# Attention on two halves of the PE array: roles exchanged once a step, and the order of the parts between

## The chip, the cores and the metric

The kernel runs on one core of one Trainium2 chip. The metric is the device time of one launch in microseconds (us), and lower is better. The core has a matrix engine (PE, with its weight loads shown apart as PEld), a vector engine (DVE), a scalar engine (ACT), GpSimd (POOL) and DMA queues, of which SP issues those of this kernel. They run at the same time and wait for each other through semaphores. The profile is of one execution.

## What is computed

One transformer block on a sequence of 2048 rows of 512: a modulation from a condition vector, a layer norm, attention with 32 query heads of 16 that share one key and one value head, a residual, a second layer norm and a gated feed-forward part of width 1792.

```python
mod = (silu(c) @ w_mod).reshape(1, 6, 1, 512)
sa, ca, ga, sb, cb, gb = ...
h = layernorm(x) * (1 + ca) + sa
q = (h @ wq)            # 32 heads of 16
k, v = h @ wk, h @ wv   # one head of 16 each
p = softmax(q @ k.T * 16 ** -0.5)
x = x + ga * (concat(p @ v) @ wo)
h = layernorm(x) * (1 + cb) + sb
x = x + gb * ((sigmoid(h @ w_gate) * (h @ w_up)) @ w_down)
```

## The kernel before

**Units and steps.** After a prologue (`PLAN`, up to line 996) the attention runs as 32 units: `units` (L544) pairs 8 blocks of 256 queries with 4 groups of 8 heads. A unit has 16 steps (`kb`, L1115), one for each block of 128 keys, so there are 512 steps. In a step the kernel computes the scores of one key block for eight heads (tiles `st`), takes Exp of them on ACT into tiles `P`, and multiplies the P of two steps earlier (`LAG` = 2) with V into one PSUM bank, `craw`, which gathers a whole unit. Beside this runs, 84 tiles ahead of 64 a unit (`A0`, L56), a second product of queries with keys (tiles `sa`), whose row maxima DVE takes; the maxima are needed for the scores of a later unit. The program's PSUM banks for these are two for `st`, three for `sa` and two for all else (`SBANKS`, L84).

**The two row halves of PE.** Query and key tiles hold two copies side by side, in partitions 0 to 63 and 64 to 127. A product for one half uses 64 rows of the array and, cut into four by `columns` (L145), its four strips of 32 columns. So one row half can compute scores while the other multiplies P with V. A step has two halves, `h` = 0 and 1 (L1128). In half `h` the products with V use rows 64`h` to 64`h`+63 (`pv`, L644; `side[0]` keeps which), and the scores use the other rows (`st_tile(i, kb, k, 1 - h)` and `a_tile`, whose odd numbers are those of rows 64 to 127). The products with V are in float32, which PE does in two rounds: 4 heads x 2 rounds = 8 `craw` matmuls a half, 16 a step.

**The order of PE's program.** All of PE's work in the loop is kept in program order (`pe` is an `Ordered`). A half issues, by `ORDER` (L57): the first `sa` tile, the first `st` tile, the products with V (`c`), the second `sa`, the second `st`; then `piece` (L1092), some terms of other work.

**The parts between.** That other work (query projections `pq`, output projection `po`, gate and up `pgu`, down `pd`) comes in couples of groups, `Couple` (L191). In its first leg group a computes with rows 0 to 63 and group c with rows 64 to 127, and in the second leg they change places, so that each group's sum over 128 rows is made in one bank. A term is one product on each row half, eight matmuls in all; `part` (L195) issues row half 0 first, then 1. `plan` and `places` (L1031) spread the terms: `RATE` 2.2 terms a half at most times, `QRATE` 0.55 and `ERATE` 1.2 earlier on; `weight` gives the last half of a unit more (`SWAP` = 5 over the rate).

**The hand-over.** Both row halves add to the one bank `craw`, and must not do so at the same time. After its products with V a half issues `hand_over` (L159): a matmul with one column of zeros (`nought`) on the rows that have just finished, in one of the four column strips in turn, which raises the semaphore `turn`. Before the next half's products with V `take_over` (L169) makes PE wait for it. In the code before, that is so at every half but a unit's first; the last half of a unit has no hand-over, since ACT then copies the bank (`unit_end`, L665, tile `cs`). A couple issues a hand-over of its own at the end of its first leg, and waits for it ahead of its second.

**What runs behind.** The maxima of a unit are finished by `max_end` and `max_rows` (L605, L612): two small reductions on DVE, a small transposing product on rows 0 to 63 of PE at the end of a step's second half, two copies on ACT, a subtraction on DVE and four DMAs from SP's queue into the query tile. The results of a unit leave by `place`, `recip` and `finish` (L680 to L712), by step counts in `defer`.

Of the kernel before, what the change touches and what calls it, by code (L numbers as in the profile page):

```python
# [26 lines left out]
NKB = S // P  # L27
# [62 lines left out]
def adaln_mqa_glu_kernel(  # L90
# [36 lines left out]
    def sbank(name):  # L127
        return psum["s"].tile([P, 512], F32, tag=name, name=name, bufs=psum["banks"][name])
# [10 lines left out]
    pe, dve, act = Ordered(nc.tensor), Ordered(nc.vector), Ordered(nc.scalar)  # L139
# [5 lines left out]
    def columns(dst, l_, r_, start, stop):  # L145
        for c_ in range(0, P, 32):
            pe.matmul(dst[c_:c_ + 32], l_[:, c_:c_ + 32], r_, start=start, stop=stop)

    turn, done, side, open_ = nc.alloc_semaphore("turn"), [0], [0], [False]
# [4 lines left out]
    def behind(later, earlier):  # L154
        tc.add_manual_dep(later.ins, earlier.ins.name,
                          mybir.DependencyInfo(mybir.DependencyClass.Sync, mybir.DependencyReason.DATA),
                          reason="a bank that Tile doesn't follow")

    def hand_over():  # L159
        g, rs = 32 * (done[0] // 2 % 4), slice(64 * side[0], 64 * side[0] + 64)  # L160
        z = pe.matmul(raw_c["c"][g:g + 32, 0:1], nought[rs], nought[rs, 0:1], start=False, stop=False)
        if not done[0]:
            behind(z, nought_set)
        done[0] += 1
        z.then_inc(turn, 1)
        tc.add_to_no_dep_group("turn", z.ins)
        tc.no_tile_sem_insts.add(z.ins.name)

    def take_over(since=None):  # L169
        pe.wait_ge(turn, done[0] if since is None else since)  # L170
# [20 lines left out]
    class Couple:  # L191
# [3 lines left out]
        def part(self, n0, n1):  # L195
            if n0 == 0:
                for g in self.gs:
                    g.open()
            m = self.gs[0].n
            for n in range(n0, n1):  # L200
                if n == m:
                    take_over(self.since)
                for j in range(2):
                    g = self.gs[j ^ (n >= m)]
                    l_, r_, *cut = g.term(n % m, slice(64 * j, 64 * j + 64))
                    columns(cut[0](g.bank) if cut else g.bank, l_, r_, n == 0, n == 2 * m - 1)
                if n == m - 1:
                    self.since = None
                    if open_[0]:
                        hand_over()  # L210
                        self.since = done[0]
            if n1 == self.n:
                for k, g in enumerate(self.gs):
                    g.end(g.bank, k == 1)
# [189 lines left out]
    V = cp.tile([P, NKB, 32], F32, name="V")  # L404
# [144 lines left out]
    Ps = {}  # L549
# [20 lines left out]
    def get_q(i):  # L570
        if i not in qps:
            b, o = units[i]
            assert (b * QU // QB, o) in qdone
            load_q(i)
        return qps[i]


    def spot(n):
        return n // 16, n // 8 % 2, n % 2, n // 2 % 4

# [19 lines left out]
    def a_tile(i, n):  # L600
        a_max(*a_product(i, n))
# [3 lines left out]
    def max_end(i):  # L605
        m16 = wp.tile([64, 32], F32, tag="m16", name="m16", bufs=4)
        for u in range(2):
            dve.tensor_reduce(m16.rearrange("p (h t u) -> p h t u", t=2, u=2)[:, :, :, u], mxs[i][64 * u:64 * u + 64],
                              axis=AX.X, op=ALU.max)
        return lambda: max_rows(i, m16)  # L610
# [17 lines left out]
        return low  # L628


    def st_tile(i, t, pr, j):
        qp = get_q(i)
        if j == 1:
            P_[pr] = P2.tile([P, 2, 512], F32, tag=f"P{pr}", name=f"P{pr}", bufs=PBUFS)
        p_ = P_[pr]
        s_ = sbank("st")
        columns(s_, kp[64 * j:64 * j + 64, t * P:(t + 1) * P], qp[64 * j:64 * j + 64, 2 * pr:2 * pr + 2].rearrange("p r q -> p (r q)"),
                True, True)
        act.activation(p_[:, j], s_, AF.Exp, scale=0.25)
        Ps[i, t, 2 * j + pr] = p_[:, j]  # L640

    def pv(i, t, j):  # L644
        c_ = raw_c["c"]
        side[0] = j
        rs = slice(64 * j, 64 * j + 64)
        if (t, j) != (0, 0):
            take_over()
        for hh in range(4):  # L650
            z = pe.matmul(c_[32 * hh:32 * hh + 32, :], V[rs, t, :], Ps[i, t, hh][rs, :],
                          start=(t == 0 and j == 0), stop=(t == NKB - 1 and j == 1))
            if (t, j, hh) == (0, 0, 0) and i > 0:
                behind(z, raw_c["out"])
        open_[0] = (t, j) != (NKB - 1, 1)
        if open_[0]:
            hand_over()
        raw_c["last"] = z
        if j == 1:
            for hh in range(4):  # L660
                del Ps[i, t, hh]
            if t == NKB - 1:
                unit_end(i)

    def unit_end(i):  # L665
        b, o = units[i]
        cs = t32("cs")
        raw_c["out"] = act.activation(cs, raw_c["c"], AF.Identity)
        behind(raw_c["out"], raw_c["last"])
        tc.declare_no_dep(raw_c["out"].ins, group="turn", reason="later matmuls into the bank stand for them")  # L670
        if i == len(units) - 1:
            last.append(cs)
            return
        lD = dr.tile([2, 8, QU], F32, tag="lD", name="lD", bufs=3)
        raw = t32("raw")
        defer(1, lambda: place(b, o, cs, lD, raw))
# [38 lines left out]
    for g in range(8):  # L715
        p_, r_, j = g // 4, g // 2 % 2, g % 2
# [65 lines left out]
    class Transposes:  # L782
        stage, n = "tr", 4

        def __init__(self, part, u):
            self.part, self.u = part, u
# [255 lines left out]
    def ready(pair, gs, i):  # L1042
        for g in gs:
            g.ready = i * NKB
        return [(pair, g) for g in gs]
# [46 lines left out]
    def piece(s, h):  # L1092
        plan(s, 2 * s + h)
        if run:
            g, n0, n1 = run.pop(0)
            if n1 > n0:
                g.part(n0, n1)


    vq = []  # L1100
    lows = []

    for i, (b, o) in enumerate(units):
        if o == 0 and b == NQ - 1:
            ends = ffn_groups(NB - 1)
            first_rows.append(Couple(*ends[0][:2]))
        if o == 0 and b % 2 == 1 and b < NQ - 1:
            blocks[b // 2] = ffn_groups(b // 2)
            wos, trs, _, es = blocks[b // 2]
            main.extend([*ready(b // 2, [Couple(*wos[:2]), trs[0], trs[2]], i), (None, len(es)), *ready(b // 2, es, i)])  # L1110
        if o == 0 and b % 2 == 0 and b > 0:
            wos, trs, gs, _ = blocks.pop(b // 2 - 1)
            gs = [Couple(*wos[2:]), trs[1], trs[3], *gs]
            main.extend([*ready(b // 2 - 1, gs[:-KEPT], i), (None, KEPT), *ready(b // 2 - 1, gs[-KEPT:], i)])
        for kb in range(NKB):  # L1115
            s = i * NKB + kb
            now[0] = s
            if kb == NKB - QLEAD - 5 and i + 2 < len(units):
                get_q(i + 2)
            late, pend[:] = pend[:], []  # L1120
            for z in [z for z in waits if z[0] <= s]:
                waits.remove(z)
                z[1]()
            rows = [max_end(*z) for z in late]
            an = A0 + 4 * s

            old, lows[:] = lows[:], []
            for h in range(2):  # L1128
                for z in ORDER:
                    k = int(z[1:] or 0)  # L1130
                    if z[0] == "a" and an + 2 * k + 1 - h < len(alist):
                        a_tile(*alist[an + 2 * k + 1 - h])
                    if z == "c" and len(vq) >= LAG:
                        pv(*vq[0], h)
                    if z[0] == "s":
                        st_tile(i, kb, k, 1 - h)
                if h == 1:
                    lows.extend(z() for z in rows)
                piece(s, h)
                if h == 0:  # L1140
                    for z in old:
                        z()
            if len(vq) >= LAG:
                vq.pop(0)
            vq.append((i, kb))
            while wdone < nw:
                if wdone < nw - 4 and (wdone + 0.5) * WSTEPS > (s + 1) * (nw - 4):
                    break
                if wdone >= nw - 4 and s < WLAST + 3 * (wdone - nw + 4):
                    break  # L1150
                wjobs[wdone]()
                wdone += 1
# [2 lines left out]
        piece(s, 1)  # L1155
    while vq:
        for n in range(2):
            pv(*vq[0], n)
        vq.pop(0)
    while waits:  # L1160
        now[0] += 1
# [55 lines left out]
```

## Time and profile before

| | us |
|---|---|
| median of 3 runs | 1693.93 |
| lowest and highest | 1693.22, 1695.38 |
| the profiled execution | 1696.61 |
| its span in the trace | 1694.8 |
| PE busy | 1657.4 (98%) |
| DVE busy | 1422.2 (84%) |
| ACT busy | 1287.2 (76%) |
| POOL busy | 610.1 (36%) |

Nearly every instruction of the loop carries line 136, that of the helper `Ordered`, so groups are told apart by their tiles: `craw<-P,V` are the products with V, `craw<-nought` the hand-overs, `sa<-kp,qp` and `st<-qp,kp` the scores, `mx<-sa` the maxima on DVE, `P<-st` the Exp on ACT. A group's row ends in its count, busy time and mean duration, and the idle time of its engine ahead of it with the releaser. A row of the view in order of time has the start, the time from there to the end of the last of its instructions, the engine, the tiles and the count; rows of different row halves and column strips overlap, and which row half a matmul uses isn't shown: it follows from the program's order and from which row half is free. The profile's durations of matmuls include their way through the array, so a row half's pace is read from the distance of starts.

### The profile page before, as it was taken

What the parts mean: (1) busy time and instruction counts of PE and PEld (TensorE: products, weight loads), DVE (VectorE), ACT (ScalarE), POOL (GpSimd) and SP (SyncE); (2) the same over time, 40 slices, a digit from 0 to 9 for tenths busy, and PEclk for the clock granted to TensorE, in tenths of its full rate; (3) what the DMA queues carried; (4) which work ended last, traced back from release to release, by engine and by line L of the source; (5) the groups of instructions that cost most, each with busy time, mean ns of one, the idle gap of its engine ahead of it and who ended that gap; (6) DMA issues with size and microseconds to landing.
All of it is one profiled execution on the core that took longest, in us unless ns stands there. A gap on an engine that the chain in (4) does not pass through costs nothing.

```text
span 1694.8 us, 88800 instructions
## 1 busy us (share of the span) xinstructions
PE 1657.4 (98%) x40227; PEld 1010.1 (60%) x40227; DVE 1422.2 (84%) x2428; ACT 1287.2 (76%) x2335; POOL 610.1 (36%) x784
## 2 busy tenths in 40 slices
PE   6999999999999999999999999999999999999998
PEld 3335555555456767666656667676667766654443
DVE  7799999999999999999999999999999999912311
ACT  5548889889888888888888888888888888884100
POOL 4432455465032442232443232223443233122423
PEclk8989999999999999999999999999999999999999
DMA  7121333321021120111121110100121110011211
GB/s 240 57 62 44 100 107 96 102 83 40 21 64 52 45 68 14 40 28 28 28 77 53 53 40 13 41 25 26 37 78 53 41 52 16 25 46 52 87 50 38
DMA packets 86726, 94.12 MB, mean 56 GB/s; under 512 B 24916, under 2 KB 65868, under 8 KB 86348
## 3 DMA queue, kind: packets, MB, share of 16 engines
q1 hardware_dynamic: 86348, 88.44, 16.7%
q8 instruction: 315, 5.16, 1.2%
q14 instruction: 63, 0.52, 0.1%
HBM read 67.82 MB, written 16.24 MB: 50 GB/s over the span
## 4 chain that ended last, share of the span: by engine, by line
PE 85%; DVE 9%; ACT 2%; DMA 1%; issue 1%; SPq 1%; POOL 1%; POOLq 0%; ACTq 0%; DVEq 0%
PE craw L136 22%; PE pgu L136 16%; PE sa L136 14%; PE st L136 12%; PE pd L136 7%; DVE mx L136 7%; PE pgu L187 5%; PE pd L187 3%; PE po L136 3%; PE pq L136 2%; ACT P L136 1%; DMA xall<-in_A_x_dram 1%; DVE st L136 1%; SPq L136 1%; DVE h2h L136 0%
## 5 line engine op out<-in xcount | busy, mean ns | idle before, releaser
L136 DVE TENSOR_REDUCE mx<-sa 128x1 f32<-128x512 f32 x2048 | 1282.8, 680 | 84.0 <-PE st L136 37.9
L136 ACT ACTIVATE P<-st 128x512 f32<-128x512 f32 x2048 | 1167.5, 597 | 215.7 <-PE st L136 150.2
L136 PE MATMUL craw<-P,V 64*32 64x512 f32 x8192 | 1093.4, 599 | 0.5 <-PE craw L136 0.2
L136 PE MATMUL sa<-kp,qp 64*32 64x512 f16 (+1 forms) x7940 | 834.1, 378 | 9.2 <-DVE mx L136 8.2
L136 PE MATMUL st<-qp,kp 64*32 64x512 f16 x8192 | 836.3, 379 | 4.3 <-ACT P L136 4.0
L136 PEld LDWEIGHTS <-kp 64*32 64x32 f16 x8192 | 337.5, 91 | 206.0 <-issue 78.3
L136 PEld LDWEIGHTS <-qp 64*32 64x32 f16 (+1 forms) x7940 | 291.7, 92 | 152.8 <-issue 73.7
L136 PE MATMUL pgu<-h2h,gw 64*32 64x512 f16 x5248 | 290.1, 376 | 0.9
L136 PEld LDWEIGHTS <-gw 64*32 64x32 f16 x7872 | 183.9, 92 | 60.2 <-issue 22.4
L136 PEld LDWEIGHTS craw<-P,V 64*32 64x32 f32 x8192 | 180.9, 105 | 18.0 <-PE craw L136 3.9
L136 PE MATMUL pgu<-h2l,gw 64*32 64x512 f16 x2624 | 177.8, 376 | 0.2 <-POOL h2l L357 0.2
L136 PE MATMUL craw<-nought 64*32 64x1 f16 x1051 | 171.3, 163 | 0.0
L898 POOL TENSOR_SCALAR th<-th 128x512 f32<-128x512 f32 x41 | 25.4, 619 | 363.5 <-ACT th L136 279.6
L136 PEld LDWEIGHTS <-nought 64*32 64x32 f16 x1051 | 97.7, 93 | 72.0 <-issue 50.9
L557 POOL MEMSET qp<- 32x1024 f16 x60 | 56.7, 944 | 86.2 <-PE st L136 67.5
L321 POOL TENSOR_SCALAR wst<-wst 128x512 f32<-128x512 f32 x46 | 28.5, 620 | 140.5 <-DMA wst<-in_B_w_up_dram 88.3
L136 PE MATMUL pd<-wdl,gh 64*32 64x512 f16 x1152 | 77.5, 376 | 0.0
L136 PE MATMUL pd<-wdh,gh 64*32 64x512 f16 x1152 | 76.6, 376 | 0.1
L136 PE MATMUL pd<-wdh,gl 64*32 64x512 f16 x1152 | 76.2, 376 | 0.0
L187 PE MATMUL pgu<-h2h,gw 128*128 128x512 f16 x240 | 71.9, 379 | 1.5 <-DVE h2h L356 1.5
L892 ACT ACTIVATE th<-pgu 128x512 f32<-128x512 f32 x15 | 9.0, 597 | 82.1 <-PE pgu L187 82.1
L136 DVE COPY u<-pgu 128x512 f32<-128x512 f32 x41 | 27.9, 681 | 49.6 <-PE pgu L136 49.1
(160 smaller groups left out, 1451.6 us busy)
## 6 DMA issues: line engine op xcount, KB each, us to landing
gw<-wD SPq DMA_DIRECT2D x56, 512.0 KB
wD<-gw SPq DMA_DIRECT2D x14, 512.0 KB
wm<-in_w_mod_dram SPq DMA_DIRECT2D x6, 1024.0 KB
qp<-qD SPq DMA_DIRECT2D x192, 32.0 KB
qD<-q SPq DMA_DIRECT2D x16, 256.0 KB
xr<-in_A_x_dram SPq DMA_DIRECT2D x16, 256.0 KB
out_dram<-ot SPq DMA_DIRECT2D x16, 256.0 KB
raw<-cs SPq DMA_DIRECT2D x248, 16.0 KB
```

The lines of the kernel that those rows point to most:

```text
L136: return (lambda *a, **k: keep(f_(*a, **k))) if pinned else f_
L187: pe.matmul(cut[0](self.bank) if cut else self.bank, l_, r_, start=(n == 0), stop=(n == self.n - 1))
L321: pool.tensor_scalar(w_, w_, SW, 0.0, op0=ALU.mult, op1=ALU.add)
L557: eng.memset(qp[j:j + 32], 0.0)
L892: act.activation(th, p_, AF.Tanh, scale=0.5 / (SH * SW))
L898: pool.tensor_scalar(th, th, 1.0, 1.0, op0=ALU.add, op1=ALU.mult)
```

## The change

In odd steps the two halves change places: `sides(t)` gives the row half of the products with V, (0, 1) in even steps and (1, 0) in odd ones. Step t ends with V on the same rows with which step t+1 begins, so the row halves change roles only between the first and the second half of a step. `hand_over` comes only after a step's first half, and `take_over` only ahead of its second. The scores follow: in each half they use the rows that V does not, so in odd steps the even-numbered `sa` tiles come first. `P` tiles are taken in a step's first half, and the first and last matmul of a unit's sum are told by the order of the halves. `Couple.part` issues, in each term, first the product of the row half that had the scores (`1 - side[0]`), then that of the other.

```diff
@@ Couple.part
-                for j in range(2):
+                for j in (1 - side[0], side[0]):
                     g = self.gs[j ^ (n >= m)]
...
+    def sides(t):
+        return (0, 1) if t % 2 == 0 else (1, 0)
...
-    def st_tile(i, t, pr, j):
+    def st_tile(i, t, pr, j, second):
         qp = get_q(i)
-        if j == 1:
+        if not second:
             P_[pr] = P2.tile([P, 2, 512], F32, tag=f"P{pr}", name=f"P{pr}", bufs=PBUFS)
...
-    def pv(i, t, j):
+    def pv(i, t, second):
         c_ = raw_c["c"]
-        side[0] = j
+        side[0] = j = sides(t)[second]
         rs = slice(64 * j, 64 * j + 64)
-        if (t, j) != (0, 0):
+        start, stop = t == 0 and not second, t == NKB - 1 and second
+        if second:
             take_over()
         for hh in range(4):
-            z = pe.matmul(c_[32 * hh:32 * hh + 32, :], V[rs, t, :], Ps[i, t, hh][rs, :],
-                          start=(t == 0 and j == 0), stop=(t == NKB - 1 and j == 1))
-            if (t, j, hh) == (0, 0, 0) and i > 0:
+            z = pe.matmul(c_[32 * hh:32 * hh + 32, :], V[rs, t, :], Ps[i, t, hh][rs, :], start=start, stop=stop)
+            if start and hh == 0 and i > 0:
                 behind(z, raw_c["out"])
-        open_[0] = (t, j) != (NKB - 1, 1)
-        if open_[0]:
+        open_[0] = not stop
+        if not second:
             hand_over()
         raw_c["last"] = z
-        if j == 1:
+        if second:
             for hh in range(4):
                 del Ps[i, t, hh]
-            if t == NKB - 1:
+            if stop:
                 unit_end(i)
...
-            for h in range(2):
+            for n, h in enumerate(sides(kb)):
                 for z in ORDER:
...
                     if z == "c" and len(vq) >= LAG:
-                        pv(*vq[0], h)
+                        pv(*vq[0], n == 1)
                     if z[0] == "s":
-                        st_tile(i, kb, k, 1 - h)
-                if h == 1:
+                        st_tile(i, kb, k, 1 - h, n == 1)
+                if n == 1:
                     lows.extend(z() for z in rows)
-                piece(s, h)
-                if h == 0:
+                piece(s, n)
+                if n == 0:
                     for z in old:
                         z()
...
         for n in range(2):
-            pv(*vq[0], n)
+            pv(*vq[0], n == 1)
```

## Prediction

> **What bounds the kernel now.** I read the page first, then the busy time by stretches, then the groups of instructions inside the longest stretch, and last the engines in order of time over two stretches of a few microseconds.
>
> ```profile
> span 1694.8 us, 88800 instructions
> PE 1657.4 (98%) x40227; PEld 1010.1 (60%) x40227; DVE 1422.2 (84%) x2428; ACT 1287.2 (76%) x2335; POOL 610.1 (36%) x784
> L136 PE MATMUL craw<-nought 64*32 64x1 f16 x1051 | 171.3, 163 | 0.0
> L136 ACT ACTIVATE cs<-craw 128x512 f32<-128x512 f32 x32 | 19.1, 596 | 8.7 <-PE craw L136 8.1
> ```
>
> PE looks full, but a PE counted as busy may have one of its two row halves idle, so the rows have to be followed singly. The stretches are cut by the kind of work beside the attention: little of it at first ("light"), much of it from 538.6 on ("heavy").
>
> ```profile
> 115.00:450.70 335.70, 329.74 (x7548) 174.97 (x7529) 323.90 (x552) 297.51 (x551) 149.38 (x191) 1.00 0.25 74
> 538.60:1504.90 966.30, 960.76 (x28223) 655.93 (x28215) 887.16 (x1489) 813.64 (x1476) 321.31 (x390) 1.00 0.14 41
> L136 PE MATMUL craw<-P,V 64*32 64x512 f32 x5377 | 719.1, 598 | 0.0
> L136 PE MATMUL st<-qp,kp 64*32 64x512 f16 x5380 | 553.1, 377 | 0.3 <-ACT P L136 0.2
> L136 PE MATMUL sa<-kp,qp 64*32 64x512 f16 x5264 | 544.5, 376 | 3.5 <-DVE mx L136 2.9 <-issue 0.5
> L136 PE MATMUL craw<-nought 64*32 64x1 f16 x700 | 114.1, 163 | 0.0
> ```
>
> The first two rows give length, then PE, PEld, DVE, ACT and POOL, and the granted clock (1.00 in both). The group rows are of the heavy stretch. A step has 16 craw matmuls, so the heavy stretch has 5377/16 = 336 steps of 966.3/336 = 2.876 us; the matmuls left over, 28223 less the four groups, are 11502, at eight to a term 4.3 terms of parts a step.
>
> Now one stretch of it in order of time, PE first and ACT after it:
>
> ```profile
> 807.52 0.41 PE L136 MATMUL sa<-kp,qp 64*32 64x512 f16 x4
> 807.60 0.63 PE L136 MATMUL craw<-P,V 64*32 64x512 f32 x4
> 807.73 0.41 PE L136 MATMUL st<-qp,kp 64*32 64x512 f16 x4
> 807.95 0.41 PE L136 MATMUL sa<-kp,qp 64*32 64x512 f16 x4
> 808.03 0.63 PE L136 MATMUL craw<-P,V 64*32 64x512 f32 x4
> 808.17 0.41 PE L136 MATMUL st<-qp,kp 64*32 64x512 f16 x4
> 808.38 0.45 PE L136 MATMUL pd<-wdl,gh 64*32 64x512 f16 x5
> 808.48 0.16 PE L136 MATMUL craw<-nought 64*32 64x1 f16 x1
> 808.48 0.40 PE L136 MATMUL pd<-wdl,gh 64*32 64x512 f16 x3
> 808.60 0.49 PE L136 MATMUL pd<-wdh,gl 64*32 64x512 f16 x8
> 808.86 0.64 PE L136 MATMUL craw<-P,V 64*32 64x512 f32 x4
> 808.89 0.42 PE L136 MATMUL sa<-kp,qp 64*32 64x512 f16 x4
> 809.10 0.42 PE L136 MATMUL st<-qp,kp 64*32 64x512 f16 x4
> ...
> 809.53 0.42 PE L136 MATMUL st<-qp,kp 64*32 64x512 f16 x4
> 809.74 0.39 PE L136 MATMUL pd<-wdh,gh 64*32 64x512 f16 x4
> 809.76 0.16 PE L136 MATMUL craw<-nought 64*32 64x1 f16 x1
> 809.77 0.40 PE L136 MATMUL pd<-wdh,gh 64*32 64x512 f16 x4
> 809.95 0.43 PE L136 MATMUL pd<-wdl,gh 64*32 64x512 f16 x8
> 810.17 0.42 PE L136 MATMUL sa<-kp,qp 64*32 64x512 f16 x4
> 810.30 0.64 PE L136 MATMUL craw<-P,V 64*32 64x512 f32 x4
> ...
> 808.19 1.26 ACT L136 ACTIVATE P<-st 128x512 f32<-128x512 f32 x2 [0.27 <-PE st L136]
> 809.63 1.14 ACT L136 ACTIVATE P<-st 128x512 f32<-128x512 f32 x2 [0.18 <-PE st L136]
> ```
>
> Score row: sa, st, sa, st start 0.215 us apart (807.52 to 808.38 is four of them), then a part of 0.215. PV row: two rounds of 0.43 (807.60, 808.03), then the hand-over matmul (nought) and the parts. So the row work of a step is 2 x 0.87 for PV, 8 x 0.215 for scores and 4.3 x 2 x 0.215 for parts, 5.31 us over two rows: 2.65 each, and 2.876 - 2.65 = 0.22 us of each step a row stands idle.
>
> Part of it is at the exchange. The score row that began at 807.52 is free at 808.60 + 0.215 = 808.815, but its PV starts at 808.86, and its first round takes 0.45 where one with weights loaded ahead takes 0.43. The hand-over was long done (808.48 + 0.16). What ends last is ACT: the first of the two Exp from 808.19 ends 0.6 later, at 808.79, and frees the bank of the next half's first st, which stands ahead of PV in the program. The next exchange is alike: free at 809.95 + 0.215 = 810.165, Exp from 809.63 to 810.23, PV at 810.30. So a score row gives way to PV **1.34** (807.52 to 808.86) or **1.41** us (808.89 to 810.30) after it began, though its work with two terms takes 6 x 0.215 = 1.29. A PV row gives way to scores after 1.31 (808.86 to 810.17), which is its work.
>
> In the light stretch the limit is another:
>
> ```profile
> 298.86 5.46 DVE L136 TENSOR_REDUCE mx<-sa 128x1 f32<-128x512 f32 x9
> L136 DVE TENSOR_REDUCE mx<-sa 128x1 f32<-128x512 f32 x512 | 314.5, 678 | 11.6 <-PE sa L136 5.1 <-PE st L136 4.7
> 303.55 0.64 PE L136 MATMUL craw<-P,V 64*32 64x512 f32 x4
> ...
> 304.28 0.40 PE L136 MATMUL st<-qp,kp 64*32 64x512 f16 x4
> 304.43 0.16 PE L136 MATMUL craw<-nought 64*32 64x1 f16 x1
> 304.44 0.40 PE L136 MATMUL sa<-kp,qp 64*32 64x512 f16 x4
> 304.86 0.40 PE L136 MATMUL st<-qp,kp 64*32 64x512 f16 x4
> 304.88 0.64 PE L136 MATMUL craw<-P,V 64*32 64x512 f32 x4
> ```
>
> DVE runs nine maxima in 5.46 us, 0.607 each, one into the other. All 512 of the light stretch need 311 us so, the rest of DVE 323.9 - 314.5 = 9.4 more: 320 of 335.7. DVE sets the pace, and PE is late for it by some 15 us in all. The rows show how: the next sa (304.44) must wait until PV has left its row (nought at 304.43), while the row that had scores stands idle from 304.28 + 0.215 to 304.88.
>
> **The change, part by part.** A step keeps its four sa, four st, 16 craw matmuls and parts; no DMA, DVE or ACT instruction is added or removed, and nothing is moved past a queue of SP or POOL.
>
> *One exchange a step instead of two, heavy stretch.* After the second half the score row goes on with scores and the PV row with PV. Per row, with two terms a half, now: 1.34 or 1.41 as score row, 1.31 as PV row, so (1.34 + 1.41 + 2 x 1.31)/4 = 1.343 a half, 2.685 a step. After: a score row takes 1.29 over the border and 1.34 or 1.41 at the exchange; a PV row 1.31 at the exchange and, over the border, 1.31 or as long as the Exp holds it (st is still ahead of PV, so PV of the new half cannot start before 1.34 to 1.41 from the beginning of the old scores; it began up to 0.09 after them, which leaves 1.31 to 1.41, say 1.34). Two steps: (1.29 + 1.34 + 1.31 + 1.34) + (1.29 + 1.41 + 1.31 + 1.34) = 10.63 over two rows and two steps: 2.658. The gain is 0.027 a step, for halves of two terms; a third term (1.51 of work) covers the wait already, and with 4.3 terms a step about one half in seven has it: 0.023 x 336 = 8 us. Of the idle 0.22, the recurrence explains only 2.685 + 0.3 x 0.215 - 2.65 = 0.10; the other 0.12 are late banks and late reductions, which at an exchange hold both rows, since each takes the other's place. Over a border they hold one. Bounds: nothing, or half of 0.12 x 336 = 20 us; I take 8, nearer the low end, because DVE (887.16 of 966.30 by the row) takes back part. Together **16**, between 0 and 37 (half of the 0.22 x 336 = 74).
>
> *The light stretch.* Over a border the next sa no longer waits for PV to leave, so half of the places where DVE starves go. Bounds 0 and 15; I take **9**, a little over half, since one half of slack also absorbs the next exchange.
>
> *Hand-over matmuls.* Of 1051, those after the second halves go: 15 in each of the 32 units, 480. Each holds one of a row's four column strips, not the row: between 808.48 and the next part in that strip lie about 0.02 us. That is 0 to 480 x 0.02 / 2 = 5 us; **2**. The wait on them goes too, at the border; at the exchange it stays. Queued behind it are sa, st and the parts of that half, as before.
>
> *Parts begin with the score row.* In the old order this was so in every second half. The score row's first part starts 0.21 after its last st either way (808.17 to 808.38, 809.53 to 809.74), so the two rows do not hold each other: **0**. If they did, the lag between the rows, 808.48 - 808.38 = 0.10, would be paid in one half a step.
>
> The Trainium skill, "TensorE: Matmul & The Clock Gate" (Part 3, what overlaps), says that matmuls start and end strictly in program order. The rows disagree: nought (808.48) stands ahead of sa (807.95) and st (808.17) in the program and starts after them. By the page's rule this part would gain up to 0.10 x 336 = 34 us; it is counted among the rivals.
>
> *Order within a step.* In odd steps the two halves change places; the maxima's four sa and the Exp come in another order, with the same counts and the same banks. At a unit's end PV's last and the next unit's first half are now on one row, and the copy of the bank (cs, 0.596) is covered as before by the five terms put there, 5 x 0.215 = 1.08: **0**; without that cover 32 x 0.6 = 19 us.
>
> *The rest* (88 us between the stretches, 47 after): **1**.
>
> Sum: 16 + 9 + 2 + 0 + 0 + 1 = 28. The profiled execution took 1696.61 us (span 1694.8); 1696.6 - 28 = 1668.6. The median of the runs, 1693.93, lies 2.7 lower, so the forecast is **1666 us**.
>
> **The rivals.** *A, the rows hold each other more than I read.* Then most of what is bounded above comes: 37 + 15 + 5 = 57, or the 34 of the part order on top of half of that: about 1637. For it: the unexplained 0.12 a step. Against: the score row's parts start on time in both orders. *B, PV is held behind scores on the border (slower).* One mechanism: over the border sa and st stand ahead of PV, and if PV's weights must wait until the score row has begun its new sa and loaded the weights of its st, PV starts about 0.12 after that sa (810.17 to 810.30 is such a distance). The PV row then loses 1.29 + 0.12 - 1.31 = 0.10 at every border whose rows lie closer than 0.12, and so does the next exchange, which waits for that row: up to 0.10 x 336 = 34, or half of it as the score row has 0.05 in hand; less the 9 and 2 above that is 6 to 23, and I take 10: 1704. It decides where the rows' lag is under 0.12. For it: 807.60 and 810.30 follow sa closely. Against: 808.86 comes ahead of sa 808.89, so PV passes scores that stand before it. *C, nothing.* ACT's Exp and DVE's maxima hold the halves as before and the saved waits only turn into waits for banks: 1692. For it: at both exchanges the Exp ended last. Against: over the border the score row needs its st bank 0.215 later than PV now feels it.
>
> **How the numbers follow.** Main case (1650 to 1685) 0.60, A 0.16, C 0.09, B 0.15. About 0.2% (3.4 us) is what a measurement can tell from no change. Faster: main, A and a quarter of C, 0.78; same: the rest of C and a little of B, 0.08; slower 0.14. The range 1640 to 1694 holds the main case, C and the nearer half of A, and leaves out B and A's far end.
>
> **What would show it.** Right: about 571 nought matmuls; heavy steps of some 2.82 us and light ones near 2.56 (now 335.7 over 512/4 = 128 steps, 2.62); at the border craw follows a part on its own row with no gap and the 0.43 spacing of its rounds; at the exchange the gap of 0.04 to 0.13 after an Exp as now. Wrong: craw at the border about 0.12 after sa with its row idle (B); DVE's maxima spaced as now with PE's gaps moved to sa (C); heavy steps under 2.75 (A). The forecast fails if the late banks, which I only bounded, make up the exchange's cost or take the gain back.

## The result, and the profile after

The changed kernel takes **1685.1 us** (median of 6 runs, 1682.68 to 1685.67), the kernel before 1695.88 (6 runs, 1693.22 to 1698.62): a ratio of 0.9933, 95% interval 0.9919 to 0.9946. It is faster, by 11 us where 28 were forecast. The page of the changed kernel, the lines that answer to those of before:

```profile
span 1683.7 us, 87854 instructions
PE 1644.5 (98%) x39747; PEld 974.6 (58%) x39747; DVE 1430.9 (85%) x2428; ACT 1295.4 (77%) x2335; POOL 610.5 (36%) x784
L136 PE MATMUL craw<-nought 64*32 64x1 f16 x571 | 93.1, 163 | 0.0
```

The change was made as described: 480 of the 1051 hand-overs are gone. The busy time by stretches, cut at the same steps as before (columns: length, then PE, PEld, DVE, ACT, POOL, the clock):

```profile
115.58:449.82 334.24, 328.43 (x7441) 165.25 (x7430) 322.96 (x552) 298.28 (x551) 149.45 (x191) 1.00 0.25 74
537.18:1495.12 957.94, 952.24 (x27908) 633.03 (x27898) 896.45 (x1489) 820.83 (x1476) 321.67 (x390) 1.00 0.14 41
```

The light stretch went from 335.7 to 334.2, the heavy one from 966.3 to 957.9, a step there from 2.876 to 2.851. So 8.4 of the 11 us come from the heavy stretch, and the light one, from which 9 were forecast, gave 1.5.

How long a row half stands idle ahead of the products with V (V for short) can be worked out from the trace, by following each of its four column strips from matmul to matmul in the order of the program and taking the mean of the four (by the distances of starts, a matmul of 512 columns keeps a strip 0.216 us, a round of V 0.429). Border is V at the beginning of a step, exchange V in its second half:

```text
idle of the row half ahead of V, us in all     light stretch        heavy stretch
                                             border  exchange     border  exchange
before                                        34.1     35.9        33.7     36.3
after                                         35.5     37.1        19.8     35.0
share of V at the border that starts 0.060 to 0.075 after the end of the Exp that
frees the bank of the first st tile (a unit's first half left out):
before 0.68 light, 0.54 heavy; after 0.88 light, 0.37 heavy
```

Though V at the border now follows V on its own row half and waits for no hand-over, it still stands behind the first st tile, and in most halves of the light stretch it starts at one fixed distance, 0.064 us, after the Exp that frees that tile's bank (in 40 of these 105 halves over 0.02 us before the st tile itself, which runs on the other row half). In the heavy stretch the idle time at the border fell by 14 us, not to nothing, and that at the exchange hardly changed. The experiments ask what these 14 us are. (Expectations below that give 22 and 32 us for the changed kernel's heavy stretch mean its 19.8 and 35.0; the sum is the same within 1 us.)

### The profile page after: what moved, and what is told of

Read it like the earlier page. It is cut to its first block, busy times and chain, and to the rows that moved or that the text cites. A ratio compares the mean times of both kernels' runs of the same rounds, so it can differ in the third digit from the quotient of the medians.

```text
span 1683.7 us, 87854 instructions
## 1 busy us (share of the span) xinstructions
PE 1644.5 (98%) x39747; PEld 974.6 (58%) x39747; DVE 1430.9 (85%) x2428; ACT 1295.4 (77%) x2335; POOL 610.5 (36%) x784
## 4 chain that ended last, share of the span: by engine, by line
PE 83%; DVE 11%; ACT 2%; issue 1%; DMA 1%; POOL 0%; SPq 0%; POOLq 0%; ACTq 0%; DVEq 0%
PE craw L136 23%; PE sa L136 16%; PE pgu L136 14%; PE st L136 10%; DVE mx L136 9%; PE pd L136 6%; PE pgu L187 5%; PE pd L187 3%; PE po L136 2%; PE pq L136 2%; ACT P L136 1%; DMA xall<-in_A_x_dram 1%; ACT th L136 1%; DVE h2h L136 1%; DVE st L136 1%
## 5 line engine op out<-in xcount | busy, mean ns | idle before, releaser
L136 PEld LDWEIGHTS <-kp 64*32 64x32 f16 x8192 | 323.9, 91 | 254.5 <-issue 102.2
L136 PEld LDWEIGHTS <-qp 64*32 64x32 f16 (+1 forms) x7940 | 284.4, 92 | 166.5 <-issue 82.4
L136 PE MATMUL pgu<-h2h,gw 64*32 64x512 f16 x5248 | 273.8, 376 | 1.0
L136 PEld LDWEIGHTS <-gw 64*32 64x32 f16 x7872 | 175.0, 92 | 59.4 <-issue 16.2
L136 PE MATMUL pgu<-h2l,gw 64*32 64x512 f16 x2624 | 165.3, 376 | 0.3 <-POOL h2l L357 0.3
L136 PE MATMUL craw<-nought 64*32 64x1 f16 x571 | 93.1, 163 | 0.0
L321 POOL TENSOR_SCALAR wst<-wst 128x512 f32<-128x512 f32 x46 | 28.5, 621 | 144.7 <-DMA wst<-in_B_w_up_dram 89.4
L136 PEld LDWEIGHTS <-nought 64*32 64x32 f16 x571 | 53.1, 93 | 34.2 <-issue 28.8
```

The costliest lines, as they stand in the source:

```text
L136: return (lambda *a, **k: keep(f_(*a, **k))) if pinned else f_
L321: pool.tensor_scalar(w_, w_, SW, 0.0, op0=ALU.mult, op1=ALU.add)
```

## The experiments

All ratios are to the kernel before, run on the same chip.

**The two parts of the change by themselves.** `parts_only` is the kernel before with the new order of a term's products; `exchange_only` is the changed kernel with the old order.

```diff
-                for j in range(2):
+                for j in (1 - side[0], side[0]):
```

> The old exchange at every half, only the order of the two products of a term changed (first the row half that had the scores). Theory of the prediction: the row halves run past each other in the program, so the order is worth nothing: time within 0.2% of before, 1692 to 1699 us. Rival (rows hold each other in program order): up to 0.10 us in each first half of the heavy stretch, faster by 10 to 30 us.

> One exchange a step, but the parts in the old order, row half 0 first. If the exchange carries the whole gain: 0.993 of before, 1683 to 1687 us, as the changed kernel. If the order of the parts carries a share: between 1687 and 1696 us.

Measured: 1695.47 us, ratio 0.9995 (0.9987 to 1.0003), and 1683.83 us, 0.9919 (0.9902 to 0.9936). The order of the parts is worth nothing, as forecast. All of the gain lies in the rest.

**Products with V ahead of the first st tile.** If the st tile's wait for its bank holds V, V can be issued ahead of it, in the changed kernel and in the one before.

```diff
-ORDER = "a0", "s0", "c", "a1", "s1"
+ORDER = "a0", "c", "s0", "a1", "s1"
```

> The changed kernel with the products with V issued ahead of the first st tile of a half (order sa, V, st, sa, st). Theory now: at the border PV is still held because the first st tile, which waits for its bank until an Exp has read it, stands ahead of V in the program; the wait for the hand-over that was taken away had not been the last one. Then the row half's idle time ahead of V at the border (now 22.0 us over the heavy stretch) falls under 8, and the time falls by 5 to 15 us against the changed kernel, to 1670 to 1680. Rival (the hand-over or the loading of weights holds V): within 3 us of the changed kernel, 1682 to 1688.

> The kernel before with V issued ahead of the first st tile. Theory now: V is freed of the Exp, and then waits for the hand-over at every half, which by the light stretch takes 0.27 us from the hand-over matmul; as that is mostly done when the row half comes free, half the gain at both places: 1685 to 1693 us. Rival: the hand-over holds V anyway and nothing changes, 1693 to 1698.

Measured: 1774.63 us (1.0463, 1.0446 to 1.0480) and 1818.92 us (1.0729, 1.0713 to 1.0745). Both expectations missed, far off. In the changed kernel V's idle time at the heavy border did fall, from 19.8 to 8.1, but the first st tile of these halves, which had 1.5 us of idle time ahead of it, now has 48. The changed kernel with V ahead, in order of time, PE and then ACT:

```profile
810.21 0.39 PE L136 MATMUL sa<-kp,qp 64*32 64x512 f16 x4
810.39 0.61 PE L136 MATMUL craw<-P,V 64*32 64x512 f32 x4
810.64 0.40 PE L136 MATMUL st<-qp,kp 64*32 64x512 f16 x4
810.82 0.61 PE L136 MATMUL craw<-P,V 64*32 64x512 f32 x4
...
811.53 0.60 ACT L136 ACTIVATE P<-st 128x512 f32<-128x512 f32 x1 [0.45 <-PE st L136]
```

The st tile ends at 810.64 + 0.40 = 811.04, and ACT stands idle until 811.53: that is 0.10 after the second round of V has ended (810.82 + 0.61 = 811.43). In the kernel before, where st stands ahead of V, the Exp of the st at 807.73 (end 808.14) began at 808.19, while V ran until 808.03 + 0.63 = 808.66. So a matmul that stands behind V in the program may start ahead of V's end, but who reads its result is released only after it: PE announces its work in the program's order. Worked out over the 978 halves that have a second sa tile: the second maximum of a half (its sa tile stands behind V) never starts earlier than 0.105 or 0.099 us after V's end in a step's two halves before, 0.104 or 0.070 after the change, and mostly 0.131 or 0.096; the first maximum (ahead of V) starts up to 1.4 us before V's end.

The trace also keeps the times at which PE raises its counters, and they show this directly. In the half of the kernel before that begins at 807.52, the second sa and st tiles end at 808.36 and 808.58, V at 808.66. The hand-over's counter rises at 808.713, and only then those of the two tiles, at 808.772 and 808.831, 0.059 us apart. In most halves the hand-over's counter rises 0.05 after V's end, and in nearly all of them PE's next raise comes 0.059 or 0.060 after that. V's own matmuls raise no counter that these readers wait on (only the last of a unit does), so it is not the counting that makes the readers wait for V.

**V behind the second sa tile.** A test of just that.

```diff
-ORDER = "a0", "s0", "c", "a1", "s1"
+ORDER = "a0", "s0", "a1", "c", "s1"
```

> The changed kernel with V issued after the second sa tile (order sa, st, sa, V, st). Theory now (PE gives its signals in program order, so what stands behind V is released only at V's end): the second maximum of a half now starts up to 0.9 us ahead of V's end, where it now never starts before V's end, and only the second Exp still follows V's end. In the changed kernel the distance from V's end to that maximum is never under 0.07 us. The time could go either way, since V now also waits for a bank of sa: 1665 to 1700. Rival (signals as each matmul ends): the maxima start as they do now, and the time is that of the changed kernel within 4 us.

Measured: the second maximum now starts up to 0.8 us ahead of V's end (median 0.05 and 0.02 ahead in a step's two halves), and only the second Exp still follows it: the signals do come in the program's order. The time is 1701.52 us, 1.0031 (1.0020 to 1.0043), just over the range given: V, now behind a bank of sa as well, stands idle 105 us in the heavy stretch instead of 55.

**DVE relieved.** Each maximum over half of the columns, and the scale of the Exp at 0.05; the output is another one.

```diff
-        dve.tensor_reduce(mxs[i][:, 4 * j + r, qt, kc:kc + 1], sa, axis=AX.X, op=ALU.max)
+        dve.tensor_reduce(mxs[i][:, 4 * j + r, qt, kc:kc + 1], sa[:, :256], axis=AX.X, op=ALU.max)
...
-        act.activation(p_[:, j], s_, AF.Exp, scale=0.25)
+        act.activation(p_[:, j], s_, AF.Exp, scale=0.05)
```

> The kernel before with DVE relieved: each maximum over 256 of the 512 columns (and the scale of the Exp 0.05 instead of 0.25, so that nothing overflows; the output is another one). Theory now: DVE is not what paces the light stretch; the results of the scores that stand behind V in the program are released only when V has ended, and V waits for an Exp, a loop of V, Exp and st banks. Then the light stretch stays within 3% of 335.7 us, and the whole is 1660 to 1692. Rival (the prediction: DVE sets the pace there): the light stretch falls by more than 25 us.

> The changed kernel with the same relief of DVE. If DVE took back the rest of the forecast gain (rival of the prediction, case C in part), the difference to the kernel before with the same relief grows from 11 us to 20 us or more. Theory now: it is not DVE, and the difference stays between 6 and 15 us.

Measured: 1675.59 us (0.9884, 0.9865 to 0.9903) and 1662.41 us (0.9801, 0.9784 to 0.9818): a difference of 13.2 us, against 11 without the relief. The light stretch of the kernel before with the relief, and its maxima there:

```profile
107.40:438.90 331.50, 325.61 (x7551) 171.30 (x7539) 208.22 (x553) 295.78 (x551) 152.98 (x197) 1.00 0.25 75
```

```profile
L136 DVE TENSOR_REDUCE mx<-sa 128x1 f32<-128x256 f32 x513 | 198.6, 420 | 122.2 <-PE st L136 109.0 <-PE sa L136 12.1 <-PE pq L136 0.5
```

DVE is busy 208.2 us instead of 323.9 and idle for 122, and the stretch is shorter by 4.2 us. DVE does not set the pace there. In the heavy stretch it took back 3 us of the gain at most: with the relief the two kernels lie 11.5 us apart there (959.0 and 947.5), without it 8.4.

**A third bank for st.** Taken from sa, which has two left.

```diff
-SBANKS = {"st": 2, "sa": 3}
+SBANKS = {"st": 3, "sa": 2}
```

> The changed kernel with three banks for st and two for sa instead of two and three. If V is held by the first st tile's wait for its bank, which an Exp must first have read, a third bank takes that wait away: the idle time of the row halves ahead of V in the heavy stretch falls from 54 us (32 at the exchange, 22 at the border) to under 25. What two banks for sa cost is open; the time may go either way, 1660 to 1720. If V's idle time stays at 45 or more, the Exp is not what holds it.

Measured: 1760.68 us, 1.0381 (1.0366 to 1.0397). This is beyond the range given, and the idle time ahead of V rose to 65 us, where under 25 was expected. By its own measure this speaks against the Exp as what holds V. But sa stands ahead of V too, and now had the wait (138 us of idle time ahead of the sa tiles, 28.5 in the changed kernel), and the trace shows that V went with it. At the light border V starts 0.055 to 0.080 after the Exp that frees the st tile's bank in 2% of the halves now (88% in the changed kernel), but 0.055 to 0.090 after the maximum that frees the sa tile's bank in 91% (9%). So V there waits for whichever of the two tiles ahead of it in the program gets its bank last.

**The hand-over put back at the border.** Rows as in the changed kernel, one exchange a step; hand-over and wait at every half (`border_handover`), or the hand-over matmul alone (`border_nought`).

```diff
-        if second:
+        if (t, second) != (0, False):
             take_over()
...
-        if not second:
+        if open_[0]:
             hand_over()
```

> The changed kernel with its exchange once a step, but with the hand-over and the wait on it at the border too, as before (1051 hand-over matmuls instead of 571). Theory now: the gain comes from the rows that no longer change places at the border, and the wait that was taken away had hardly ever been the last one, since V is held until the first st tile has its bank from an Exp: at most 4 us lost, 1684 to 1689. Rival (the prediction's own count of hand-overs and of the wait): most of the gain is lost, 1691 to 1697.

> The changed kernel with the hand-over matmul issued after the second halves too (1051 of them), but with no wait for it at the border. Theory now: the gain was neither the exchange nor the wait but the matmul itself: PE gives its signals in program order, the hand-over matmul stands between V and the second sa and st, and so holds back the second maximum and the second Exp of its half by some 0.035 us (V's end to the maximum 0.131 with it, 0.096 without). Then the time goes back to 1691 to 1697. Rival (the wait at the border): it stays at 1683 to 1687.

Measured: 1695.82 us, 0.9994 (0.9984 to 1.0003), and 1684.96 us, 0.9940 (0.9924 to 0.9957). My theory fell in both, the rival was right. With hand-over and wait put back, the whole gain is gone: that the row halves no longer change places at the border is worth nothing that can be measured. With the matmul alone put back the gain stays: the 480 matmuls cost 1 us by the ratios, within the intervals. **What the change gains is the wait.**

**A later hand-over**, behind the second st tile, so that it does not stand between V and the second sa and st.

```diff
-            hand_over()
+            owed.append(1)    # paid after the half's last st tile
```

> The changed kernel with the hand-over matmul issued after the second st tile of the half instead of right after V. Theory now: in the first halves too the second maximum starts 0.096 us after V's end instead of 0.131, and the time falls by 4 to 10 us, to 1675 to 1681. Rival (the wait is what costs): the hand-over comes no earlier, and the time is 1683 to 1688.

> The kernel before with the hand-over matmul issued after the second st tile, at every half, with all its waits and exchanges. Theory now: that alone gives at least the gain of the change: 1676 to 1687 us. Rival (the wait at every half is what costs): 1692 to 1698.

Measured: 1682.26 us (0.9922, 0.9908 to 0.9937) and 1704.28 us (1.0053, 1.0035 to 1.0070). Both expectations missed. The second maximum does start 0.035 us earlier, but in the changed kernel that gives 2 to 3 us, within the intervals, and the kernel before becomes slower. From there, in order of time:

```profile
303.24 0.40 PE L136 MATMUL st<-qp,kp 64*32 64x512 f16 x4
303.46 0.40 PE L136 MATMUL pq<-h1l,wdh 64*32 64x512 f16 x4
303.48 0.16 PE L136 MATMUL craw<-nought 64*32 64x1 f16 x1
303.48 0.40 PE L136 MATMUL pq<-h1l,wdh 64*32 64x512 f16 x4
303.69 0.41 PE L136 MATMUL sa<-kp,qp 64*32 64x512 f16 x4
303.87 0.63 PE L136 MATMUL craw<-P,V 64*32 64x512 f32 x4
```

V begins 0.39 after the hand-over's start, where 0.26 lies between the two in the kernel before (678.23 to 678.49, below): the matmul runs as early as ever, but its signal now comes behind those of the sa and of the st that ends at 303.64. By the counters it rises 0.17 after V's end instead of 0.05, two signals of 0.059 later, and V starts 0.043 after it at the earliest, in both. From the time at which V's second round frees its row half (0.429 after that round's start) to the next V lie, in the light stretch, never less than 0.276 us in the kernel before and 0.393 here, and here in 80% of the halves hardly more than that. So the wait is last at some places, and at which ones was still open.

**Which waits.** V's `take_over` waits for all hand-overs so far. A couple of parts issues one of its own when its first leg ends, and that stands behind the couple's last part, next to the following V. In the kernel before, 59 halves have one ahead of V, 31 of them at a border. The same border (step 1 of a unit), before and after the change:

```profile
677.59 0.57 PE L136 MATMUL pd<-wdl,gh 64*32 64x512 f16 x5
677.79 0.16 PE L136 MATMUL craw<-nought 64*32 64x1 f16 x1
...
677.83 0.58 PE L136 MATMUL pd<-wdh,gl 64*32 64x512 f16 x7
678.22 0.38 PE L136 MATMUL sa<-kp,qp 64*32 64x512 f16 x1
678.23 0.16 PE L136 MATMUL craw<-nought 64*32 64x1 f16 x1
678.24 0.39 PE L136 MATMUL sa<-kp,qp 64*32 64x512 f16 x3
678.43 0.41 PE L136 MATMUL st<-qp,kp 64*32 64x512 f16 x4
678.49 0.63 PE L136 MATMUL craw<-P,V 64*32 64x512 f32 x4
```

```profile
675.67 0.47 PE L136 MATMUL pd<-wdh,gl 64*32 64x512 f16 x8
675.89 0.42 PE L136 MATMUL sa<-kp,qp 64*32 64x512 f16 x4
675.95 0.16 PE L136 MATMUL craw<-nought 64*32 64x1 f16 x1
675.96 0.61 PE L136 MATMUL craw<-P,V 64*32 64x512 f32 x4
```

Before: V's own hand-over at 677.79, the parts, the couple's hand-over at 678.23, and V 0.26 after it. After: the couple's hand-over at 675.95 and V 0.01 behind it, right as its row half comes free. Two kernels put the wait back at the one kind of border and at the other (`mine` is the count at V's own last hand-over):

```diff
-        if second:
+        if second or t > 0 and done[0] != mine[0]:    # border_wait_others: ==
             take_over()
```

> One exchange a step, hand-over matmuls at every half, and at the border a wait only where a couple ended its first leg in the piece just before (31 of the 480 borders). Theory now: the wait of V counts every hand-over so far, so also that of a couple, which comes only after the couple's last part; there V, and all that stands behind it in the program, starts about 0.3 us late, and 31 x 0.3 = 9 us is the whole gain of the change. Then these 31 waits alone bring the time back to 1691 to 1697 us. Rival (the wait for V's own hand-over costs a little at each border): 1683 to 1688.

> The same with a wait at the other 449 borders and none at those 31. Theory now: V's own hand-over is done long before V can start (0.276 us after V's end, while two terms keep the row half 0.43): 1683 to 1688 us. Rival: 1691 to 1697.

Measured: 1693.29 us, 0.9990 (0.9976 to 1.0004), and 1687.02 us, 0.9963 (0.9950 to 0.9976). Against 0.9940 with no wait at the border, the 31 waits behind a couple cost 8.3 us by the medians (8.5 by the ratios), the other 449 between 2 (medians) and 4 (ratios), with intervals that overlap. In the profiles it is plainer: the heavy stretch is 958.8 us with no wait, 959.0 with the 449, 964.0 with the 31, 964.9 with all. The border of above with the couples' wait:

```profile
676.08 0.48 PE L136 MATMUL pd<-wdh,gl 64*32 64x512 f16 x8
676.30 0.41 PE L136 MATMUL sa<-kp,qp 64*32 64x512 f16 x4
676.38 0.16 PE L136 MATMUL craw<-nought 64*32 64x1 f16 x1
676.51 0.41 PE L136 MATMUL st<-qp,kp 64*32 64x512 f16 x4
676.64 0.63 PE L136 MATMUL craw<-P,V 64*32 64x512 f32 x4
```

V stands 0.26 behind the couple's hand-over again, with the rows of the changed kernel.

**The wait without the couples' share**, in both kernels: V waits for V's own hand-over alone, and a couple's hand-over ahead of an exchange goes to the row half that takes V next.

```diff
                     if open_[0]:
-                        hand_over()
+                        if crossing[0]:
+                            take_over(mine[0])
+                        hand_over(side[0] ^ crossing[0])
...
-            take_over()
+            take_over(mine[0])
```

> The changed kernel with V waiting for V's own hand-over alone, not for a couple's; a couple's hand-over ahead of an exchange goes to the row half that is to take V next. Theory now: the 28 couples that end their first leg in a step's first half still make V late at the exchange by 0.3 us each (their mean idle ahead of V is 0.35 us, the others' 0.08 in the heavy stretch); 28 x 0.28 = 8 us: 1673 to 1680. Rival: no change, 1683 to 1687.

> The kernel before, exchange at every half and all waits kept, with the same change of count alone. Theory now: all 59 late starts go, 59 x 0.28 = 16 us: 1675 to 1685, as fast as the changed kernel or faster. Rival (the exchange itself is worth something): not under 1690.

Measured: 1682.12 us (0.9924, 0.9908 to 0.9941) and 1686.13 us (0.9953, 0.9938 to 0.9968). The first lies above the range expected, the second 1 us above it. The kernel before, with an exchange, a hand-over and a wait at every half as ever, gains 9.3 us by the medians (8.0 by the ratio), most of what the change gains, from this edit alone. In the heavy stretch the mean idle time ahead of V behind a couple's hand-over is:

```text
                     border (24 halves)   exchange (25 halves)   the other halves
before                     0.390                0.301              0.078, 0.092
after                      0.050                0.352              0.060, 0.084
before_own_count           0.075                0.097              0.069, 0.082
after_own_count            0.050                0.099              0.060, 0.087
```

The step that I expected is there at all places, and the other halves changed by 0.02 at most. Of the 14 us that left the heavy border, the 24 halves behind a couple make up 8. But the time fell by less: 9.3 us for 59 late starts (16 expected), and in the changed kernel 28 late starts went from the trace for some 3 us (8 expected), within the intervals. The late start of one row half is partly made good by the other; how much, these runs do not settle.

**Both small gains together**, with the changed kernel beside it: V's own count, and V's hand-over behind the second st.

> The changed kernel once more, beside the next one on the same chip: 0.993 of before, 1682 to 1688 us.

> The changed kernel with V waiting for V's own hand-over alone and with that hand-over issued after the second st tile. If both small gains add up (the couples' late starts at the exchange, 3 us by medians, and the second maximum 0.035 us earlier in each first half, 3 us): 0.989 to 0.992 of before, 1677 to 1682 us. Rival: the later hand-over is now the last thing ahead of V, as it was in the kernel before, and takes the first gain back: 0.992 to 0.994.

Measured: 1684.44 us (0.9930, 0.9917 to 0.9943) and **1677.47 us** (0.9891, 0.9876 to 0.9907). The two add up, to a version that is 18 us faster than the kernel before and 7 faster than the changed one.

## Where the prediction was right, and where it was wrong

**Direction and place.** Faster, and by the heavy stretch: right. That the 8.4 us of the heavy stretch lie between the bounds of 0 and 37 is luck, since they came by another way than the one forecast. The steps there are 2.85 us, not 2.82, and in the light one 2.61, not 2.56.

**"One exchange a step instead of two, heavy stretch": 16, and "The light stretch": 9.** Both wrong, in size and in mechanism. The run with the exchange halved and the waits kept is at 0.9994 of before (0.9984 to 1.0003), 1 us (3 at the most) where these two terms made 25. Over the border I let PV begin "1.31 or as long as the Exp holds it" and took 1.34; the profile shows that in the light stretch 88% and in the heavy 37% of these halves still start at the fixed distance after the Exp. The row halves no longer change places, but V stands behind the same st tile in the program as ever, and whatever is late in one row half still holds the other by that order. For the light stretch the step that failed is "DVE sets the pace": back-to-back maxima, with 15 us of slack, were read as the bound, but with 116 us less of DVE work the stretch was 4 us shorter. An engine that is busy nearly all the time need not be the one that sets the pace; what does so in the light stretch these runs do not show.

**The step that carried the gain was priced at nothing.** The prediction says that "the hand-over was long done" at the exchange and then only that the wait "goes too, at the border". That was read from V's own hand-over, in two exchanges of which neither had a couple ending in it. Of the 1051 hand-overs the 59 of the couples stand next to the following V, and the wait counts them too: 31 places at the border, some 0.3 us each, 8.3 us by the run that puts back these alone. The count to be made was 1051 - 992 = 59 (992 from 31 of each unit's 32 halves), and what each of the 59 stands ahead of.

**"Hand-over matmuls": 2.** In range for the matmuls themselves; the run with all of them back differs from the changed kernel by less than its interval. **"Parts begin with the score row": 0.** Right, 0.9995.

**The rivals.** *A* and *B* didn't come: at the heavy border V's row half stands idle for 0.06 us on average, not the 0.12 of B, and nothing became slower. *C*, that ACT's Exp holds the halves as before, describes the exchange's own worth well; what it left out is the wait. The rule of the Trainium skill that I set against the rows ("TensorE: Matmul & The Clock Gate", Part 3: matmuls start and end in program order) was half of it: starts do not keep the order here (nought, at 677.79, stands ahead of the parts at 677.59 in the program), but the release of readers does (never before V's end, over 978 halves). I read the first and let the second go with it; it is what holds the second maximum and the second Exp of a half to V's end.

**What stays open.** Why a late start of V of 0.3 us costs 0.27 us of the run at the border, but about 0.16 over all 59 places; and what sets the pace of the light stretch. V's wait for the banks of the tiles ahead of it, and those tiles' wait for Exp and maxima, make a loop that would fit, but no run takes it apart.

## What to carry to other kernels

A wait on a counter waits for everything that was ever counted on it: before pricing it, list who adds to the counter and take the adder that stands closest ahead of the waiter, not the one it is meant for. Where one gain has several parts, a run that keeps the headline change and puts back only the small one (here a wait) tells more than any recurrence. And an engine that is busy all through a stretch is shown to be its bound only if relieving it shortens the stretch by about as much.

## What the runs showed of the hardware

Matmuls on different row halves start out of the program's order, by up to 0.87 us in the heavy stretch, but what waits for them is released in the program's order, with 0.059 us from one signal of PE to the next: a maximum or an Exp behind V in the program never began earlier than 0.07 us after V's end, and moving V ahead of one st tile cost the changed kernel 89 us (1685.1 to 1774.63). A matmul of one column of zeros costs next to nothing by itself (480 of them: 1 us by the ratios, within the intervals), while a wait for it ends some 0.26 us after its start, and 0.39 when two score tiles stand ahead of it in the program.
